# Moving half of the memory sums into the feed-forward sweep, and giving the last two batch pairs a sweep each

## The chip, the cores and the metric

One core of one Trainium2 chip runs the whole program. The metric is device time in microseconds (us) of one execution. PE is the matrix engine, DVE the vector engine, ACT the scalar engine, POOL the GpSimd engine, SP the engine that issues the transfers. Each engine works through its own instructions strictly in the order of the program; between engines there are only semaphores.

## The reference

Eight batches, eight heads, 576 tokens, 64 dimensions, 32 memory slots. An attention over memory slots, then a gated feed-forward layer (512 to 1536 to 512) on all 4608 tokens:

```python
a = exp(phi - max(phi, axis=seq)); a = a / (sum(a, axis=seq) + 1e-9)
k_m = einsum('bhsm,bhsd->bhmd', a, k)
v_m = einsum('bhsm,bhsd->bhmd', a, v)
s = q @ k_m.T / sqrt(64)
attn = softmax(s); out = attn @ v_m          # one row of 512 per token: x
xn = x / sqrt(mean(x * x) + 1e-6) * rms_g
g = xn @ w_gate; val = xn @ w_val
return (g * sigmoid(g) * val) @ w_out
```

The three weights arrive as 64-bit floats, everything else as 32-bit ones.

## The kernel before, in words

**Splitting.** The large products are made from values split into a high and a low part, each in a format that PE reads at full rate: high by high, high by low, low by high, three matmuls for one. A split is a cast on ACT (the high part: xh, hh, ath, wh, oh) and a subtraction on DVE or POOL (the low part: xl, hl, atl, wl, ol).

**Weights.** `convert` turns a block of 64-bit weights (128 x 512, tile raw) into 32-bit ones with integer steps on DVE: the exponent (tile ex, L345 to L358), the mantissa (tile mi, L365, L369), their product (tile w, L385); one activation on ACT and the split stand between. There are 36 blocks, named by kind and number: 0 is gate, 1 value, 2 output. Each split block is also written to DRAM, and `reload` fetches it from there when it is needed again.

**Batches in pairs.** Pair 0 holds batches 0 and 1, and so on to pair 3; pairs 2 and 3 are the late batches 4 to 7.

**Part 1** (up to line 819) makes k_m and v_m of all eight batches: the max of phi over tokens (mc, L509; transposed as mt on PE, L516; max mx; transposed back as mr, L533; subtracted, L542), the exponential into e_bd, its products with keys and values (kvp, L583) and with ones (L598), the division, and transposes (kvt). POOL adds several of the exponentials first (es), so that fewer products with ones are needed. For pairs 0 and 1 it also makes the queries' transposes (qtp), the scores (S, L718), the attention a, and the norm: `x_steps` transposes a (tp, L184), multiplies by a Gram matrix of v_m (xp, L235), sums on DVE (L248), takes the inverse root in 25 small DVE steps (`fin`, L259 to L276), and spreads the result over the transposed attention (rp on PE, L204, and L212 on DVE). The late batches' v_m and Gram matrices go to DRAM.

**Part 2** has 48 iterations, one for each block of 128 hidden columns and each pair. An iteration multiplies v_m with the gate and value block (vp, L852, 12 matmuls; evacuated as xh on ACT and xl on DVE), multiplies the attention with the result (pg and pv, L888, 48 matmuls; silu sg on ACT, product hf on DVE, hh on ACT, hl on POOL), and after every second iteration adds the output block for nine token tiles (po, L930, 54 matmuls; sum acc on DVE, first by a copy, L935, then by an addition, L937). Sweep 1, the first 24 iterations, takes pairs 0 and 1 in turn; sweep 2 takes pairs 2 and 3 in turn, with the weights read back once. Inside sweep 1 lie most of the weight conversions, the eight attention steps (`attend_steps`) of pairs 2 and 3, and the norms of both.

**Order.** Every step has a number, its place in iterations, from a table (`PRM`): `ev` collects pairs of place and function, sorts them and calls them. From that trace a scheduler sets each engine's order, which is then fixed. PSUM, eight banks, is given out by pools; part 2's tiles take the banks that part 1 gives back.

## Time and profile before

| | |
|---|---|
| runs, median (lowest to highest) | 919.43 us (917.98 to 920.09) |
| profiled execution, its span | 921.27 us, 919.5 us |
| PE busy | 843.9 us, 92% |
| DVE busy | 633.7 us, 69% |
| ACT busy | 382.2 us, 42% |
| POOL busy | 287.7 us, 31% |
| moved by DMA | 106.41 MB, mean 116 GB/s |

PE reads as busy while one of its matmuls is in flight, also where the next has to wait a little; so the share of 92% does not mean that only 8% could be saved. A row of the timeline gives start, duration, engine, line, operation and tiles, and in brackets the idle time ahead of it with what ended it. A row of a group gives the count, the total, the mean of one in ns, and the idle time ahead.

### The profile page before, as it was taken

How to read it: one execution, taken by the hardware profiler on the slowest of the kernel's cores; microseconds unless marked ns; L12 is line 12 of the kernel's file. 1: busy time of each engine (PE TensorE's matmuls, PEld its weight loads, DVE VectorE, ACT ScalarE, POOL GpSimd, SP SyncE). 2: the span in 40 equal slices, each digit the busy share in tenths (PEclk: the TensorE clock that was granted, in tenths of full speed). 3: DMA queues.
4: the chain of work that ended last, by engine and by line, in shares of the span. 5: the costliest groups of instructions: out<-in, count | busy, mean ns of one | idle time of the engine just before them, and what ended most of it. 6: DMA issues, size and time to landing. Idle time of an engine off the chain costs nothing.

```text
span 919.5 us, 15815 instructions
## 1 busy us (share of the span) xinstructions
PE 843.9 (92%) x6207; PEld 750.0 (82%) x6207; DVE 633.7 (69%) x1094; ACT 382.2 (42%) x647; POOL 287.7 (31%) x242
## 2 busy tenths in 40 slices
PE   4899675799989999999999999999999999999997
PEld 3778664788878798888887897799989999999996
DVE  5587969998998978978964664655455454554543
ACT  2566333645545445555542352333324233242330
POOL 3465735331432332333332151222111121121120
PEclk9799876999999999999999999999999999999999
DMA  8997644443353423433323135221203012040046
GB/s 281 268 292 244 224 138 130 135 160 82 126 165 104 158 88 120 133 109 126 116 76 115 35 92 150 69 81 47 93 1 118 20 47 92 1 138 1 1 112 141
DMA packets 85666, 106.41 MB, mean 116 GB/s; under 512 B 38996, under 2 KB 56920, under 8 KB 85592
## 3 DMA queue, kind: packets, MB, share of 16 engines
q1 hardware_dynamic: 85592, 105.41, 37.8%
q8 instruction: 49, 0.80, 0.4%
q14 instruction: 25, 0.20, 0.1%
HBM read 73.93 MB, written 31.46 MB: 115 GB/s over the span
## 4 chain that ended last, share of the span: by engine, by line
PE 59%; DVE 14%; issue 5%; ACT 3%; POOL 1%; DVEq 0%; ACTq 0%; POOLq 0%
PE po L930 26%; PE pv L888 13%; PE pg L888 13%; PE vp L852 5%; DVE xl L866 2%; DVE mi L369 1%; DVE hf L897 1%; DVE w L385 1%; DVE acc L937 1%; DVE ex L352 1%; DVE ex L345 1%; DVE mi L365 1%; DVE ex L358 1%; DVE ex L357 1%; DVE acc L935 1%
## 5 line engine op out<-in xcount | busy, mean ns | idle before, releaser
L911 POOL TENSOR_TENSOR hl<-hf,hh 128x512 fp32r<-128x512 f32 (+1 forms) x96 | 139.9, 1457 | 441.8 <-ACT hh L910 439.5
L937 DVE TENSOR_TENSOR acc<-po,acc 128x512 f32<-128x512 f32 x180 | 123.1, 687 | 117.2 <-PE po L930 116.3
L930 PE MATMUL po<-oh,hh 128*128 128x512 f32 x432 | 173.4, 402 | 4.8 <-DVE ex L1005 1.9
L930 PE MATMUL po<-oh,hl 128*128 128x512 f32 x432 | 171.3, 397 | 0.0
L930 PE MATMUL po<-ol,hh 128*128 128x512 f32 x432 | 171.1, 396 | 0.0
L896 ACT ACTIVATE sg<-pg 128x256 f32<-128x256 f32 x192 | 77.4, 409 | 170.4 <-PE pg L888 146.4
L866 DVE TENSOR_TENSOR xl<-vp,xh 64x1024 fp32r<-64x1024 f32 x96 | 117.0, 1219 | 39.0 <-ACT xh L865 37.6
L865 ACT CAST xh<-vp 64x1024 fp32r<-64x1024 f32 x96 | 96.7, 1007 | 68.3 <-PE vp L852 31.3
L897 DVE TENSOR_TENSOR hf<-pv,sg 128x256 f32<-128x256 f32 x192 | 84.4, 452 | 51.3 <-PE pv L888 39.6
L910 ACT CAST hh<-hf 128x512 fp32r<-128x512 f32 (+1 forms) x96 | 64.7, 673 | 105.2 <-DVE hf L897 63.7
L888 PE MATMUL pg<-ath,xh 128*128 128x320 f32 (+1 forms) x384 | 86.3, 300 | 13.0 <-ACT xh L865 8.0
L930 PEld LDWEIGHTS po<-oh,hl 128*128 128x128 f32 x432 | 81.6, 189 | 19.5
L930 PEld LDWEIGHTS po<-oh,hh 128*128 128x128 f32 x432 | 82.0, 190 | 18.7 <-DVE acc L937 3.0
L930 PEld LDWEIGHTS po<-ol,hh 128*128 128x128 f32 x432 | 82.0, 190 | 11.3
L852 PE MATMUL vp<-wh,vm 128*128 128x256 f32 x384 | 86.3, 290 | 2.6 <-DVE xl L866 1.6
L888 PE MATMUL pv<-ath,xh 128*128 128x320 f32 (+1 forms) x384 | 85.1, 302 | 2.7 <-DVE hf L897 2.6
L888 PE MATMUL pg<-ath,xl 128*128 128x320 f32 (+1 forms) x384 | 85.0, 296 | 0.0
L888 PE MATMUL pg<-atl,xh 128*128 128x320 f32 (+1 forms) x384 | 84.6, 296 | 0.0
L888 PE MATMUL pv<-atl,xh 128*128 128x320 f32 (+1 forms) x384 | 84.3, 297 | 0.0
L888 PE MATMUL pv<-ath,xl 128*128 128x320 f32 (+1 forms) x384 | 83.8, 298 | 0.0
L888 PEld LDWEIGHTS pg<-ath,xh 128*128 128x128 f32 x384 | 63.7, 190 | 18.9 <-ACT xh L865 8.3
L852 PEld LDWEIGHTS vp<-wh,vm 128*128 128x128 f32 x384 | 66.9, 195 | 5.7 <-DVE xl L866 2.0
(131 smaller groups left out, 1393.8 us busy)
## 6 DMA issues: line engine op xcount, KB each, us to landing
kv<-in_k_dram SPq DMA_DIRECT2D x32, 288.0 KB, 6.3
kv<-in_v_dram SPq DMA_DIRECT2D x32, 288.0 KB, 6.5
out_dram<-acc SPq DMA_DIRECT2D x72, 128.0 KB, 2.4
raw<-in_moe_w_gate_dram SPq DMA_DIRECT2D x12, 512.0 KB, 3.8
raw<-in_moe_w_val_dram SPq DMA_DIRECT2D x12, 512.0 KB, 3.7
wd<-wh SPq DMA_DIRECT2D x12, 512.0 KB, 3.3
wd<-wl SPq DMA_DIRECT2D x12, 512.0 KB, 3.5
raw<-in_moe_w_out_dram SPq DMA_DIRECT2D x12, 512.0 KB, 3.6
```

The lines of the kernel that those rows point to most:

```text
L345: V.tensor_scalar(out=ex, in0=hw, scalar1=0x7FF00000, scalar2=None, op0=ALU.bitwise_and)
L352: V.tensor_scalar(out=ex, in0=ex, scalar1=float(-896 << 20), scalar2=0.0, op0=ALU.add, op1=ALU.max)
L852: nc.tensor.matmul(vp[:, cc, e, :], lhs(l), r[:, 2 * cc + e, :], start=(n == 0), stop=(n == 2),)
L865: nc.scalar.copy(xh[rows], src)
L866: nc.vector.tensor_tensor(out=xl[rows], in0=src, in1=xh[rows].bitcast(F32), op=ALU.subtract)
L888: nc.tensor.matmul(pt[:, :N], l[:, cc, b, half * P:half * P + P], r[:, b, cc, t0:t0 + n, :].rearrange("p t x -> p (t x)"), start=(m == 0), ...
L896: nc.scalar.activation(sg[:, :N], pg[:, :N], AF.Silu)
L897: nc.vector.tensor_tensor(out=hf[:, :, b, :], in0=pv[:, :N].rearrange("p (t x) -> p t x", x=64), in1=sg[:, :N].rearrange("p (t x) -> p t x ...
L910: nc.scalar.copy(hh, hv)
L911: nc.gpsimd.tensor_tensor(out=hl, in0=hv, in1=hh.bitcast(F32), op=ALU.subtract)
L930: nc.tensor.matmul(po, l[:, tt, :], r, start=(m == 0), stop=(m == 5))
L937: nc.vector.tensor_tensor(out=accs[key], in0=po, in1=accs[key], op=ALU.add)
```

## The change

Part 1 now handles pairs 0 and 1 only. The late batches' key and value sums are a new function, `late_kv`, of 19 steps, placed at iterations 1.5, 3.8, 13.5 and 15.5 of sweep 1. It works in two PSUM buffers (tag o) that the attention steps use as well, and in SBUF tiles of those steps.

The iterations are dealt anew: pairs 0 and 1 share the first 24, then pair 2 has twelve, then pair 3. The weights are read back twice. The attention steps of pair 3 and its norm move into pair 2's sweep.

Two pieces of work go to ACT: one step of each conversion's exponent (`CB`), and the copy that starts each sum (`accs`). POOL's es sums are gone from part 1 (`ESN`), all sums over tokens are made by products with ones there. The loads of part 1 stand in a fixed list. The first PSUM tiles of part 2 are asked for in the order o, v, vw. From the end of pair 0's norm on, later DVE steps are held behind it (`issue_after`). The tile w2 of the conversions has two buffers in place of three.

```diff
-WB = 3
+WB = 2
-    K_AT=[12.08, 15.05, 41.68, 67.52, 100.72, 122.69, 147.6, 167.28],
+    K_AT=[12.0, 21.0, 50.0, 60.0],
-    ESN=[3, 3, 2, 3, 3, 3, 2, 3],
+    ESN=0,
-    SU=[1.874, 3.014, 5.716, 6.6, 9.746, 12.208, 13.357, 15.533],
+    WR=2.85,
+    OR=0.4,
+    KV=[1.5, 3.8, 13.5, 15.5],
+    SU=[6.0, 7.6, 9.2, 10.8, 24.2, 25.7, 27.2, 28.7],
-    XB=[17.199, 22.916],
+    XB=[18.0, 30.2],
-    CB=0,
+    CB=1,
...
-        for b in range(B):
+        for b in range(2 * G):
             steps, post = kv_steps(b)
...
             ev += [(PRM["X_AT"][pr] + PRM["XP"] * p, f) for p, f in x_steps(
-                    pr, lambda t, pr=pr: a_tiles[pr][:, t], tile_of("tr"), tile_of("kx"))]
+                pr, lambda t, pr=pr: a_tiles[pr][:, t], tile_of("tr"), tile_of("tr" if pr else "kx"))]
         for _, f in sorted(ev, key=lambda e: e[0]):
-            f()
+            with tc.issue_after(roots[0]) if 0 in roots else nullcontext():
+                f()
+    ps.tile([P, 512], F32, tag="o", name="o_first")
+    ps.tile([P, 512], F32, tag="v", name="v_first")
+    ps.tile([P, 2, 2, 256], F32, tag="vw", name="vw_first", bufs=1)
+    UNITS = [(p, u) for u in range(NU) for p in range(G)] + [(p, u) for p in range(G, NP) for u in range(NU)]
     def where(i):
-        ps_, r = divmod(i, NU * G * 2)
-        u, r = divmod(r, G * 2)
-        pi, f = divmod(r, 2)
-        return ps_, u, ps_ * G + pi, 2 * u + f
+        pr, u = UNITS[i // 2]
+        j = 2 * u + i % 2
+        return u, pr, j, j if pr < G else NJ * (pr - G + 1) + j
...
                 if u == 0:
-                    nc.vector.tensor_copy(accs[key], po)
+                    nc.scalar.copy(accs[key], po)
...
+    def late_kv(b):
...
+        def top():
+            d["mc"] = mc = sb.tile([P, HP, M], F32, tag="la", name=f"mc{b}")
+            nc.vector.tensor_reduce(
+                out=mc, in_=d["phi"].rearrange("p hp c m -> p hp m c"), axis=AX.X, op=ALU.max
+            )
+        def turn_mc():
+            d["t"] = tp = o_tile(f"mt{b}")
+            nc.tensor.transpose(out=tp[:, :P], in_=d["mc"].rearrange("p hp m -> p (hp m)"), identity=ident)
...
+        def exp():
+            for h in range(2):
+                rows = slice(64 * h, 64 * h + 64)
+                nc.scalar.activation(late[pr][rows, :, :, 32 * h:32 * h + 32], d["phi"][rows], AF.Exp)
...
+        def mm(cc):
+            def f():
+                d["kvp"] = kvp = o_tile(f"kvp{b}_{cc}")
...
+        return [
+            lambda: (fetch_phi(), fetch_kv(0)()), top, turn_mc, top2, turn_mb, less, exp, some,
+            mm(0), sums(0), norm(0), fetch_kv(1), mm(1), sums(1), norm(1), turn, post, self_products, post2,
+        ]
...
+        if n >= NJ:
+            ev.append((i - PRM["WR"], lambda n=n: reload(0, n)))
+            ev.append((i - i % 2 - PRM["OR"] + 0.01 * (i % 2), lambda n=n: reload(2, n)))
+    for a, p in enumerate(PRM["KV"]):
+        ev += place(p, PRM["KO"], late_kv(2 * G + a))
```

Three places show what this does to the engines' order. A row is line, operation, tiles and shape; the first digit in a tile's name is the pair, the batch or the iteration, in ex, mi and w it is the kind and the next one the block. The first place is DVE at the end of part 1, in pair 1's inverse root (rinv1, u1). Before:

```order
L274 TENSOR_TENSOR u1_1666<-rinv1_71 128x9
L275 TENSOR_TENSOR u1_1666<-u1_1666,m1_1660 128x9
L276 SCALAR_TENSOR_TENSOR rinv1_71<-u1_1666,rinv1_71 128x9
...
L212 TENSOR_TENSOR at1_1503<-at1_1503,rp1_0_1760 128x1024
L212 TENSOR_TENSOR at1_1503<-at1_1503,rp1_4_1770 128x1024
L385 TENSOR_TENSOR w1_1_1735<-mi1_1_1731,ex1_1_1726 128x512
L212 TENSOR_TENSOR at1_1503<-at1_1503,rp1_8_1776 128x256
L345 TENSOR_SCALAR ex2_0_1828<-raw_20_1724 128x512
...
L385 TENSOR_TENSOR w2_0_1839<-mi2_0_1833,ex2_0_1828 128x512
L866 TENSOR_TENSOR xl0_1823<-vp0_1809,xh0_1822 64x1024
```

and with the change:

```order
L358 SCALAR_TENSOR_TENSOR ex2_1_1614<-raw_21_1285,ex2_1_1614 128x512
L986 TENSOR_REDUCE mc4_1695<-phi4_1656 128x128
L276 TENSOR_TENSOR u1_1401<-u1_1401,m1_1395 128x9
L385 TENSOR_TENSOR w2_1_1631<-mi2_1_1625,ex2_1_1614 128x512
L277 SCALAR_TENSOR_TENSOR rinv1_75<-u1_1401,rinv1_75 128x9
L345 TENSOR_SCALAR ex0_2_1714<-raw_02_1481 128x512
L365 TENSOR_SCALAR mi0_2_1719<-raw_02_1481 128x512
L275 TENSOR_TENSOR u1_1401<-rinv1_75 128x9
L347 TENSOR_SCALAR ex0_2_1714<-ex0_2_1714 128x512
L369 SCALAR_TENSOR_TENSOR mi0_2_1719<-raw_02_1481,mi0_2_1719 128x512
```

The root's steps, which stood together, now have conversions and a late batch's max between them; the conversion that stood behind the root is gone from there.

The second place is PE, from the end of pair 1's norm to the first gate matmul. Before:

```order
L204 MATMUL rp1_8_1776<-ident_58,rinv1_71 128x128
L652 MATMUL kvt7_1755<-vt7_1766 64x64 x4
L852 MATMUL vp0_1809<-wh0_1363,vm0_456 128x256
L852 MATMUL vp0_1809<-wl0_1364,vm0_456 128x256
...
L888 MATMUL pg0_00_1849<-ath0_1393,xh0_1822 128x256 x2
```

and with the change:

```order
L205 MATMUL rp1_8_1425<-ident_58,rinv1_75 128x128
L850 MATMUL vp0_1454<-wh0_554,vm0_388 128x256
L850 MATMUL vp0_1454<-wl0_555,vm0_388 128x256
L850 MATMUL vp0_1454<-wh0_554,vm0_388 128x256 x2
...
L850 MATMUL vp0_1454<-wh0_554,vm0_388 128x256
L992 MATMUL mt4_1747<-ident_58,mc4_1695 128x128
L886 MATMUL pg0_00_1494<-ath0_883,xh0_1467 128x256 x2
```

The first v_m product stands directly behind the spreading of the norm in both; batch 7's transposes have left, and batch 4's first one has come in ahead of the gate matmul.

The third place is DVE in sweep 1, at iterations 7 and 8. Before:

```order
L897 TENSOR_TENSOR hf6_1_3012<-pv6_10_3014,sg6_10_3027 128x5x64
L897 TENSOR_TENSOR hf6_1_3012<-pv6_11_3062,sg6_11_3075 128x5x64
L866 TENSOR_TENSOR xl8_3143<-vp8_3045,xh8_3142 64x1024
L385 TENSOR_TENSOR w2_5_3476<-mi2_5_3470,ex2_5_3459 128x512
L897 TENSOR_TENSOR hf7_0_3123<-pv7_00_3125,sg7_00_3138 128x4x64
L345 TENSOR_SCALAR ex0_6_3571<-raw_06_3225 128x512
L365 TENSOR_SCALAR mi0_6_3587<-raw_06_3225 128x512
L897 TENSOR_TENSOR hf7_0_3123<-pv7_01_3177,sg7_01_3190 128x4x64
L352 TENSOR_SCALAR ex0_6_3571<-ex0_6_3571 128x512
L369 SCALAR_TENSOR_TENSOR mi0_6_3587<-raw_06_3225,mi0_6_3587 128x512
L866 TENSOR_TENSOR xl8_3143<-vp8_3045,xh8_3142 64x1024
L937 TENSOR_TENSOR acc0_0_2109<-po5_0_2874,acc0_0_2109 128x512
```

and with the change:

```order
L358 SCALAR_TENSOR_TENSOR ex0_5_2735<-raw_05_2592,ex0_5_2735 128x512
L385 TENSOR_TENSOR w0_5_2762<-mi0_5_2741,ex0_5_2735 128x512
L345 TENSOR_SCALAR ex1_5_2798<-raw_15_2676 128x512
L365 TENSOR_SCALAR mi1_5_2811<-raw_15_2676 128x512
L347 TENSOR_SCALAR ex1_5_2798<-ex1_5_2798 128x512
L864 TENSOR_TENSOR xl8_2890<-vp8_2802,xh8_2889 64x1024
L369 SCALAR_TENSOR_TENSOR mi1_5_2811<-raw_15_2676,mi1_5_2811 128x512
L935 TENSOR_TENSOR acc0_0_1760<-po5_0_2625,acc0_0_1760 128x512
L358 SCALAR_TENSOR_TENSOR ex1_5_2798<-raw_15_2676,ex1_5_2798 128x512
L864 TENSOR_TENSOR xl8_2890<-vp8_2802,xh8_2889 64x1024
L385 TENSOR_TENSOR w1_5_2817<-mi1_5_2811,ex1_5_2798 128x512
L345 TENSOR_SCALAR ex2_4_2929<-raw_24_2744 128x512
```

Both have conversions there. Before, one step or two of a conversion stand between the sweep's own rows; now parts of three conversions follow one another, with the two halves of xl8 among the steps of one.

262 lines of the change are left out of this document (179 added, 83 removed).

## The prediction

> **What bounds the kernel now.** I read the windows view first, with the span cut where the matmuls change their rate: up to the first gate matmul, the first sweep in three pieces, its tail, the second sweep, the end.
>
> ```profile
> core 0: us, PE busy (x) PEld busy (x) DVE busy (x) ACT busy (x) POOL busy (x), PEclk, DMA share, GB/s
> 0.00:158.10 158.10, 114.78 (x1485) 97.77 (x1485) 115.86 (x240) 71.04 (x128) 80.26 (x87) 0.85 0.74 222
> 158.10:292.10 134.00, 119.60 (x832) 109.07 (x833) 125.81 (x202) 71.28 (x118) 43.18 (x31) 0.97 0.43 132
> 292.10:319.40 27.30, 23.17 (x147) 19.26 (x146) 26.88 (x44) 12.58 (x19) 10.86 (x8) 0.94 0.53 170
> 319.40:539.80 220.40, 214.88 (x1470) 190.45 (x1469) 171.43 (x305) 106.76 (x181) 73.51 (x58) 1.00 0.32 101
> 539.80:603.20 63.40, 60.28 (x395) 52.00 (x394) 35.02 (x75) 19.25 (x34) 18.12 (x17) 0.97 0.43 111
> 603.20:900.00 296.80, 296.80 (x1825) 270.13 (x1824) 151.19 (x222) 100.53 (x167) 60.20 (x42) 1.00 0.18 56
> 900.00:919.50 19.50, 14.41 (x63) 11.33 (x61) 7.52 (x12) 0.79 (x2) 1.57 (x1) 0.97 0.66 153
> ```
>
> From 603.2 to 900 us PE never idles, so there a matmul's price is the distance from its start to the next one's. The timeline of that stretch has it:
>
> ```profile
> 700.07 0.39 PE L930 MATMUL po<-oh,hh 128*128 128x512 f32 x1
> 700.30 0.39 PE L930 MATMUL po<-ol,hh 128*128 128x512 f32 x1
> 703.56 0.28 PE L852 MATMUL vp<-wh,vm 128*128 128x256 f32 x1
> 703.68 0.29 PE L852 MATMUL vp<-wl,vm 128*128 128x256 f32 x1
> ```
>
> po 0.2325, vp 0.119 and, from the same view, gate and value 0.131 us on average: the 588 po (three groups like the first below), 1009 gate and value and 228 vp in that window make 296, its length. The groups of that window (first row), and of the first sweep's:
>
> ```profile
> L930 PE MATMUL po<-oh,hl 128*128 128x512 f32 x196 | 77.4, 395 | 0.0
> ...
> L930 PE MATMUL po<-oh,hh 128*128 128x512 f32 x182 | 73.7, 405 | 4.7 <-DVE ex L1005 1.9 <-DVE acc L937 1.9 <-ACT qT L982 0.9
> L888 PE MATMUL pg<-ath,xh 128*128 128x256 f32 (+1 forms) x192 | 44.4, 305 | 13.0 <-ACT xh L865 8.0 <-ACT sg L896 5.0
> L852 PE MATMUL vp<-wh,vm 128*128 128x256 f32 x192 | 42.0, 292 | 1.6 <-DVE xl L866 1.6
> ```
>
> In the first sweep 546 po (three such groups) cost 127, 1152 gate and value (six) 151, 288 vp (192 and 96) 34, and 23 for the late batches' scores and norm sums: 335. The sweep takes 381.7, so 46 us are lost, though PE reads as busy for 357.7. By piece the loss is 24 of the first 134.0 us (PE work 110), 7 of the next 27.3 (20) and 15 of the last 220.4 (206). DVE is busy 94%, 98% and 78% of these pieces: where it is full PE waits, and where its work is 171.4/206 = 0.83 of PE's, 7% of PE's time is still lost. After the sweep 8, 1 and 5.4 us are lost.
>
> So the span is 158 to the first gate matmul, 701 of PE work, and 46 + 8 + 1 + 5.4 of loss: 919.5. The profiled run took 921.3, the median of the runs is 919.4; I put the sum for the span down as the time of a run.
>
> Before 158.1 us PE does 84 us of work by such prices. What sets its end, in the timelines:
>
> ```profile
> 97.28 0.22 PE L718 MATMUL S<-km,qT 128*64 128x64 f32 x1
> 120.68 1.97 PE L184 MATMUL tp<-ident,a 128*128 128x128 f32 x8
> 138.41 0.17 DVE L259 TENSOR_SCALAR m<-ssq 128x9 f32<-128x9 f32 x1
> 142.56 0.17 DVE L276 SCALAR_TENSOR_TENSOR rinv<-u,rinv 128x9 f32<-128x9 f32 x1
> 147.23 0.58 PE L852 MATMUL vp<-wh,vm 128*128 128x256 f32 x1 [0.87 <-DVE at L212]
> 149.61 1.49 DVE L352 TENSOR_SCALAR ex<-ex 128x512 int32<-128x512 int32 x1
> 155.82 1.21 DVE L866 TENSOR_TENSOR xl<-vp,xh 64x1024 fp32r<-64x1024 f32 x1
> 158.12 0.80 PE L888 MATMUL pg<-ath,xh 128*128 128x256 f32 x2 [7.96 <-ACT xh L865]
> 158.43 0.41 DVE L352 TENSOR_SCALAR ex<-ex 128x512 int32<-128x512 int32 x1
> ```
>
> A chain: pair 1's last score, 23 us to its attention a, 18 us of transposes and norm sums, 4.2 us of inverse root, then 15.5 us to the gate matmul. In the last stretch one weight conversion stands ahead of xl on DVE, with steps of 1.49 us that take 0.41 at 158.43.
>
> **The change part by part.** *Late batches leave part 1.* One batch costs PE 72 kvp at 0.060, four transposes, self products, two max transposes and sums: 4.3 + 0.8 + 0.45 + 0.6 + 0.3 = 6.4 us (rows of the kind below; 2.94/49 = 0.060). Four batches, 25.6 us, go from a stage where PE is half idle into one where it is the floor: PE work after the first gate matmul becomes 701 + 26 = 727.
>
> ```profile
> 93.41 2.94 PE L583 MATMUL kvp<-kv,e_bd 128*64 128x128 f32 x49
> L509 DVE TENSOR_REDUCE mc<-phi 128x128 f32<-128x1152 f32 (+1 forms) x9 | 17.3, 1936 | 7.8 <-DMA phi<-in_phi_dram 7.8
> L542 DVE TENSOR_TENSOR phi<-phi,mr 128x1152 f32<-128x1152 f32 (+1 forms) x9 | 11.0, 1218 | 11.2 <-PE mr L533 11.2
> 146.26 5.96 POOL L224 TENSOR_TENSOR atl<-at,ath 128x512 fp32r<-128x512 f32 x4
> ```
>
> The change pays, then, only as far as the first gate matmul comes earlier than 158.1 and the losses behind it shrink: 26 us have to be won.
>
> *The first gate matmul.* Loads bound it from below: 16 of 32 key and 16 of 32 value loads of 288 KB and four phi go, about 12 MB of 35 in this stretch, and the rest, 23 MB at 222 to 264 GB/s, needs some 90 to 105 us. Pair 1's last scores follow its last query and the late key blocks, which stand behind pair 0's norm sums in PE's order; I put them at 99, about where they are now. From there to a took 23 us while DVE was busy 20 of 21 us and POOL ran sums for late batches; without those, 12 to 23, taken 14: 113. Transposes and norm sums took 18 with late batches' matmuls between them; alone, with two PSUM buffers instead of four, 14: 127. Then the inverse root: its 25 small steps took 4.2 in a row, but DVE's new order (the first of the three places shown above) holds between them the rest of the first output block, three whole conversions and the max of batch 4. A conversion's six steps cost 3 x 0.42 + 3 x 0.68 = 3.3 where nothing disturbs DVE (row at 158.43 for the short kind), so 0.7 + 3 x 3.3 + 2.2 + 4.2 = 17: 144. Nothing may start without it, since the rows behind it on PE are rp1 and vp0. Against that the conversion no longer stands ahead of xl0: rp, vp0, two halves of xh and one of xl, 1.3 + 2.5 + 2.0 + 1.2 with waits, is 9 where it was 15.5. **First gate matmul at 153**, bounds 140 (a at 105, three conversions waiting for their loads elsewhere) and 162 (23 us to a, phi of batch 4 late, which DVE meets in the middle of the root).
>
> *DVE in the first sweep.* It now does 324 us there (125.8 + 26.9 + 171.4):
>
> ```profile
> L937 DVE TENSOR_TENSOR acc<-po,acc 128x512 f32<-128x512 f32 x73 | 49.9, 684 | 30.1 <-PE po L930 29.8
> L385 DVE TENSOR_TENSOR w<-mi,ex 128x512 f32<-128x512 f32 x31 | 27.7, 894 | 2.2 <-POOL wl L403 0.7 <-POOL ol L403 0.7
> L369 DVE SCALAR_TENSOR_TENSOR mi<-raw,mi 128x512 f32<-128x512 uint32 x31 | 26.6, 858 | 0.0
> L357 DVE TENSOR_SCALAR ex<-ex 128x512 int32<-128x512 int32 x31 | 18.6, 601 | 0.0
> L352 DVE TENSOR_SCALAR ex<-ex 128x512 int32<-128x512 int32 x31 | 18.3, 591 | 0.0
> L935 DVE COPY acc<-po 128x512 f32<-128x512 f32 x18 | 12.2, 677 | 0.1
> L1017 DVE TENSOR_REDUCE sm<-ex 128x18 f32<-128x576 f32 x8 | 6.0, 749 | 2.2 <-ACT ex L1012 2.1
> ```
>
> A conversion of seven steps is 153/31 = 4.9 us. One step of 0.6 goes to ACT in each, and about four conversions now come before the sweep: 27 x 4.35 = 117, 36 less. The 18 first copies, 12.2, go to ACT. Four of eight attends leave, 13 (each 4 steps of 0.45 and 0.75 + 0.54 + 0.26). Each late batch brings a max 2.2, a subtraction 1.35 and some 3 of small steps: four make 25, after the part of batch 4 that lies earlier. 324 - 36 - 12 - 13 + 25 = 288. PE work in the sweep becomes 335 - 8 (four attends) + 26 = 353. DVE stands at 288/353 = 0.82 of PE's work, as in the last piece now, which lost 7%: **25 us**. On top: the conversions no longer lie evenly. One w2 buffer fewer and the new events leave iterations 4 to 7 without one and put six between hf7 and hf8 (the third place shown begins there). Four such clumps follow, 26 to 34 us of DVE against 15 to 18 of PE; the one piece of that kind now, 292.1 to 319.4, lost 7. Half of that pattern is in the 7% already; I add 6: **31**. From below 20 (only the clumps cost, at half of 7 each, and 6), from above 42, where each clump costs DVE's excess less about 5 us for which PE has other rows.
>
> ACT takes 27 activations of 0.63 and 18 copies of about 0.7, 30 us, and stands at 191 of 382 now: I cost that at nothing, hidden by ACT's own idle half, though hh is queued behind them, and po waits for hh.
>
> *Sweeps of pairs 2 and 3.* Weights are read back twice instead of once; one iteration moves 1.5 MB in 14 us, 107 GB/s, where 222 was reached: hidden. Four attends and pair 3's norm now lie in pair 2's sweep, which has DVE half free; the 9 us lost after 539.8, mostly for pair 3's norm, become 6 (bounds 3 and 12). The tail stays at 5.4.
>
> **Sum:** 153 + 727 + 31 + 6 + 5.4 = 922, against 919.4: the gain in part 1 and on DVE, 23 us, is eaten by the 26 us that move under PE's floor.
>
> **The rivals.** *Faster, 904.* The clumps run undisturbed. The mechanism is POOL against DVE: while POOL splits at in one row of 5.96 us from 146.26, a DVE step takes 1.49, otherwise 0.41. If POOL is quiet in the clumps, six steps cost 3.3 instead of 4.35, 27 conversions 28 us less, and DVE at 260/353 loses about 18 instead of 31; with part 1's chain undisturbed as well, the gate matmul comes at 148. 148 + 727 + 18 + 6 + 5.4 = 904. For it: the low row; against: POOL splits each conversion's result and two hl per iteration in the same clumps, and the mean of such a step over the sweep is 0.6, not 0.4. It decides from 20 us of loss down. The Trainium skill (SBUF — State Buffer, Who interferes with whom) says that DVE steps with two SBUF inputs, or in a two-port mode, contend with GpSimd for a shared port pair, one blocking the other; the rows of 1.49 beside 0.41 agree.
>
> *Clearly slower, 938.* Late batches as they behaved in part 1: each is a chain mc, mt, mx, mb, mr, exp, kvp, kvt in PE's in-order queue, and whatever stands behind waits too.
>
> ```profile
> PE mt L516 <- DVE mc L509: 10.0, 3, 5.0
> PE mr L533 <- DVE mb L528: 6.4, 4, 3.8
> L1012 ACT ACT_TABLE_LOAD x8 | 10.3, 1283 | 0.8 <-issue 0.4 <-DVE ex L1005 0.2
> ```
>
> 3.3 for a mt and 1.6 for a mr is 5 for each batch, 16 to 20 in all: 922 + 16 = 938. For it: mt4 stands directly ahead of the first gate matmul. Against: iterations lie between a step and its matmul, as far as the order shows. It decides if PE's waits name mt, mr, kvp or kvt with more than 2 us per batch. Each late batch also costs ACT two table loads around its exp, 1.28 each. The Trainium skill (ScalarE: Activation LUTs, What ACT_TABLE_LOAD costs) gives 1.28 us and a drain of 1.38 more for a switch; the row has the first part, and no row here shows the second. By it eight switches would take ACT 21 us instead of 10.
>
> *The dealt banks do nothing.* vp waited 0.87 us for DVE at L212. That is all the order of the PSUM pools can win at the start, and it is inside the 9 us above.
>
> **How the numbers follow.** 45% for the forecast, which spreads from 912 to 932 with the start of the sweep; 30% for the faster rival and what lies below; 25% for the slower. A change of 0.2%, 1.8 us, can be told from none. Of the forecast's band a little over a quarter lies below 917.6 and as much within 1.8 us of 919.4: faster 0.30 + 0.12, same 0.12, slower 0.25 + 0.21. Range: earliest gate matmul with the small loss, 140 + 727 + 20 + 6 + 5.4 = 898, and the latest with the large, 162 + 727 + 42 + 6 + 5.4 = 942; both ends at once are unlikely, and the low one more so than the slower rival: 901 to 942.
>
> **What would show it.** The first pg at 150 to 156, with the inverse root's first and last rows 15 us apart on DVE. The first sweep's 24 iterations 375 to 395 long, DVE busy under 80% of it, long iterations at 8 to 9 and 12 to 13. No wait over 5 us from a late batch's tile. From iteration 24 on 14 us each. I am wrong if the gate matmul comes before 145, if the sweep loses under 20, or if pair 2's sweep waits for reloaded weights.

## The result, and the profile after: 979 us, ratio 1.064

The changed kernel took 979.17 us (median, 975.72 to 980.36) beside 919.76 for the kernel before on the same chip: ratio 1.0637, 95% interval 1.0613 to 1.0662. Slower was forecast as about as likely as faster, but by 2 us and at most 22, not by 59. Times here are of fast executions alone; one slow execution of experiment 9's first kernel, of 2102 us, is not counted. The profiled execution has a span of 978.6 us; its windows, cut at the first gate matmul, at iteration 24 (end of sweep 1) and at the ends of the other two sweeps:

```profile
core 0: us, PE busy (x) PEld busy (x) DVE busy (x) ACT busy (x) POOL busy (x), PEclk, DMA share, GB/s
0.00:168.40 168.40, 104.51 (x1206) 89.34 (x1206) 98.67 (x229) 66.00 (x120) 46.49 (x61) 0.71 0.53 163
168.40:587.90 419.50, 384.48 (x2714) 340.77 (x2715) 302.86 (x500) 216.62 (x359) 142.36 (x107) 0.96 0.38 123
587.90:785.20 197.30, 192.63 (x1333) 171.27 (x1332) 104.70 (x187) 86.91 (x142) 48.14 (x37) 0.99 0.46 136
785.20:960.90 175.70, 175.70 (x1063) 159.40 (x1063) 82.76 (x123) 63.32 (x106) 37.87 (x29) 1.00 0.31 98
960.90:978.60 17.70, 12.92 (x57) 10.13 (x55) 7.05 (x11) 0.73 (x1) 1.57 (x1) 0.94 0.60 134
```

With the prediction's prices for a matmul the PE work in the last four windows is 353, 185, 175 and 13. What is left of each is loss:

| | before | forecast | after | after less forecast |
|---|---|---|---|---|
| first gate matmul | 158.1 | 153 | 168.4 | +15.4 |
| PE work from there on | 701 | 727 | 726 | -1 |
| loss in sweep 1 | 46 | 31 | 66.5 | +35.5 |
| loss behind it | 14.4 | 11.4 | 17.7 | +6.3 |
| span | 919.5 | 922 | 978.6 | +56 |

So the PE work was sized rightly. The miss is the loss in sweep 1, and the gate matmul, which came later than before instead of earlier. Its chain in the timeline (PE and DVE rows):

```profile
115.30 1.27 PE L712 MATMUL S<-km,qT 128*64 128x64 f32 x36 [0.30 <-ACT qT L699]
126.07 1.12 PE L185 MATMUL tp<-ident,a 128*128 128x128 f32 x4 [9.51 <-POOL a L752]
143.80 0.17 DVE L260 TENSOR_SCALAR m<-ssq 128x9 f32<-128x9 f32 x1
148.36 2.08 DVE L986 TENSOR_REDUCE mc<-phi 128x128 f32<-128x1152 f32 x1
158.32 0.16 DVE L277 SCALAR_TENSOR_TENSOR rinv<-u,rinv 128x9 f32<-128x9 f32 x1
158.63 1.94 PE L205 MATMUL rp<-ident,rinv 128*128 128x128 f32 x8 [15.40 <-DVE rinv L277]
161.21 0.47 PE L205 MATMUL rp<-ident,rinv 128*128 128x128 f32 x1 [0.64 <-DVE at L213]
161.34 0.56 PE L850 MATMUL vp<-wh,vm 128*128 128x256 f32 x1
168.45 0.79 PE L886 MATMUL pg<-ath,xh 128*128 128x256 f32 x2 [4.09 <-ACT xh L863]
```

From pair 1's last score (the last start in the first row's group, 116.3) to the gate matmul it is 52.1 us; the prediction had 54 (14 + 14 + 17 + 9; measured 9.8, 17.7, 14.5 and 10.1). All of the error lies ahead of these rows: the last score came at 116.3, not at 99. The longest wait of the queue that issues the loads (total, count, longest), and then rows of that queue and of DVE:

```profile
SPq L299 <- PE kvp L583: 38.5, 3, 33.4
```
```profile
75.44 0.33 SPq L299 DMA_DIRECT2D kv<-in_k_dram  x1
78.30 14.44 SPq L299 DMA_DIRECT2D q<-in_q_dram  x8
92.79 0.59 SPq L299 DMA_DIRECT2D raw<-in_moe_w_gate_dram  x1
98.58 0.43 DVE L345 TENSOR_SCALAR ex<-raw 128x512 int32<-128x512 int32 x1 [11.61 <-DMA raw<-in_moe_w_gate_dram]
105.43 0.42 DVE L615 TENSOR_TENSOR kb<-kvp,im 128x256 f32<-128x256 f32 x1
```

The queue stands for 33.4 us, from 42.0 to 75.4: batch 3's keys wait for a buffer that batch 2's kvp frees, and that kvp stands behind pair 0's norm sums on PE. So pair 1's queries go out from 78 on and the weight block at 92.8. DVE waits for that block with batch 3's division behind it, and makes one conversion and half of the next before it divides (kb, at 105.43); batch 3's transposes and pair 1's scores follow. Batch 3's own products end on PE only at 99.2, since its keys were late, so of this delay some 6 us are DVE's.

In sweep 1 PE's waits are spread, and none is large:

```profile
PE pv L886 <- DVE hf L895: 11.2, 5, 3.6
PE pg L886 <- ACT xh L863: 4.7, 3, 4.1
...
PE kvp L1030 <- ACT e_late L1015: 2.1, 2, 1.3
```

Listing for each matmul how much later the next one starts than its price allows, 40 of the 66 us are steps over 0.4 us (before: 28 of 46), and 26 are many small ones (18). How a stall makes some of the second kind is seen where pv waited longest, in the timeline of POOL, DVE and PE:

```profile
273.95 2.03 POOL L909 TENSOR_TENSOR hl<-hf,hh 128x640 fp32r<-128x640 f32 x1
275.92 2.02 POOL L966 MEMSET e_late<- 128x2304 f32 x1
274.59 3.64 DVE L345 TENSOR_SCALAR ex<-raw 128x512 int32<-128x512 int32 x1
278.15 1.48 DVE L365 TENSOR_SCALAR mi<-raw 128x512 int32<-128x512 int32 x1
280.62 0.40 DVE L895 TENSOR_TENSOR hf<-pv,sg 128x256 f32<-128x256 f32 x1
276.12 0.46 PE L886 MATMUL pg<-ath,xl 128*128 128x320 f32 x2
281.07 0.90 PE L886 MATMUL pv<-ath,xh 128*128 128x320 f32 x2 [3.62 <-DVE hf L895]
281.77 0.73 PE L886 MATMUL pv<-atl,xh 128*128 128x320 f32 x2
```

This is the clump between iterations 7 and 8, just ahead of the third place of the order shown above, whose first row stands at 286.04. One conversion step takes 3.64 us in place of 0.41, for as long as POOL runs a split and then clears e_late, a tile that the change added; hf stands behind it on DVE and PE behind hf. Seven of the profiled kernels have this order, and the step takes 3.63 to 3.64 us in each. After 3.6 us of idleness PE's next matmuls take 0.73 a pair where the same shape took 0.46. The slow stretch is longer than the stall: a vp at 286.57 still takes 0.41, one at 287.12 takes 0.29. The granted clock from the stall on is 0.66:

```profile
177.00:277.50 100.50, 94.73 (x727) 86.00 (x725) 60.63 (x86) 60.22 (x99) 39.62 (x28) 0.98 0.30 99
277.50:285.90 8.40, 4.83 (x19) 4.79 (x20) 8.40 (x19) 3.40 (x7) 3.31 (x3) 0.66 0.52 158
```

Two pages of the Trainium skill bear on these rows. The Trainium skill (SBUF — State Buffer, Who interferes with whom) says that a DVE step in a two-port mode and a GpSimd instruction exclude each other, whichever starts first, for the whole instruction; the step of 3.64 us ends 0.3 us after POOL's second instruction (275.92 + 2.02), which agrees. The Trainium skill (TensorE: Matmul & The Clock Gate, Part 1) says that the array's clock falls to half after an idle window of about 3.4 us and comes back after a busy one as long. These rows agree with the fall, with 3.6 us of idleness ahead of the slow pairs; the way back took longer here, since the vp at 286.57 is slow 5.5 us after PE's restart at 281.07.

### The profile page after: what moved, and what is told of

It reads as the page before. It is cut to its first block, busy times and chain, and to the rows that moved or that the text cites. A ratio compares the mean times of both kernels' runs of the same rounds, so it can differ in the third digit from the quotient of the medians.

```text
span 978.6 us, 16269 instructions
## 1 busy us (share of the span) xinstructions
PE 870.2 (89%) x6367; PEld 770.9 (79%) x6367; DVE 596.0 (61%) x1048; ACT 433.6 (44%) x725; POOL 276.4 (28%) x232
## 4 chain that ended last, share of the span: by engine, by line
PE 64%; DVE 19%; ACT 6%; DMA 4%; issue 4%; POOL 1%; SPq 1%; DVEq 0%; ACTq 0%; POOLq 0%
PE po L928 26%; PE pv L886 12%; PE pg L886 12%; PE vp L850 5%; DVE xl L864 3%; PE xp L236 2%; DVE ex L345 2%; DVE acc L935 2%; DVE w L385 2%; DVE mi L365 2%; DVE ex L358 1%; DVE ex L347 1%; DVE mi L369 1%; PE tp L185 1%; ACT xh L863 1%
## 5 line engine op out<-in xcount | busy, mean ns | idle before, releaser
L894 ACT ACTIVATE sg<-pg 128x256 f32<-128x256 f32 x192 | 78.3, 411 | 162.4 <-PE pg L886 132.5
L928 PE MATMUL po<-oh,hh 128*128 128x512 f32 x324 | 132.1, 408 | 7.7 <-DVE ex L1155 3.1
L928 PE MATMUL po<-ol,hh 128*128 128x512 f32 x324 | 129.7, 400 | 0.0
L928 PE MATMUL po<-oh,hl 128*128 128x512 f32 x324 | 129.0, 399 | 0.0
L886 PE MATMUL pv<-ath,xh 128*128 128x320 f32 (+1 forms) x384 | 86.4, 306 | 11.2 <-DVE hf L895 11.2
L850 PE MATMUL vp<-wh,vm 128*128 128x256 f32 x384 | 83.8, 291 | 3.1 <-DVE xl L864 1.6
L886 PE MATMUL pg<-atl,xh 128*128 128x320 f32 (+1 forms) x384 | 86.3, 300 | 0.0
L928 PEld LDWEIGHTS po<-oh,hh 128*128 128x128 f32 x324 | 61.9, 191 | 21.0 <-DVE acc L935 4.7
L886 PEld LDWEIGHTS pv<-ath,xh 128*128 128x128 f32 x384 | 64.9, 194 | 16.4 <-DVE hf L895 11.4
L928 PEld LDWEIGHTS po<-oh,hl 128*128 128x128 f32 x324 | 61.8, 191 | 14.5
```

The source lines that it names most:

```text
L850: nc.tensor.matmul(vp[:, cc, e, :], lhs(l), r[:, 2 * cc + e, :], start=(m == 0), stop=(m == 2),)
L886: nc.tensor.matmul(pt[:, :N], l[:, cc, b, half * P:half * P + P], r[:, b, cc, t0:t0 + n, :].rearrange("p t x -> p (t x)"), start=(m == 0), ...
L894: nc.scalar.activation(sg[:, :N], pg[:, :N], AF.Silu)
L928: nc.tensor.matmul(po, l[:, tt, :], r, start=(m == 0), stop=(m == 5))
```

## The experiments

Four theories were in play: the late batches cost more in the sweep than their matmuls (theirs), the conversions come in clumps because w2 has two buffers (clumps), the two moves to ACT cost more than ACT's idle half (ACT), and part 1 is held up by its new order, in the loads or on DVE (order). All medians stand beside about 920 for the kernel before and 979 for the change. Experiments 1 to 3 have two executions each, the others four to ten. A time within a profile is of one execution: over five kernels whose part 1 is nearly that of the kernel before (its own, three of experiment 6 and that of experiment 5), the first gate matmul lies between 155.4 and 159.9, so differences of 4 us there are not clear of chance.

**1. The change without the late sums.** They are left out (zeros stand for them), everything else stays.

```diff
+        return [filled]
...
-        ev += place(p, PRM["KO"], late_kv(2 * G + a))
+        ev += place(p, PRM["KO"][:1], late_kv(2 * G + a))
```

`filled`, the only step left, writes the zeros.

> The changed kernel without the late batches' sums: their k_m, v_m and Gram matrices are set to zero, so the sums, their loads, exponentials and transposes are left out. PE work falls by 25.6 us, DVE's by 25, ACT's by about 20. Theory C (clumps): the sweep is 419.5 - 26 = 394 with a loss of 60 or more. Rival K (late batches): the loss goes back to 45 or less, the sweep takes 372 to 380, the run 930 to 940.

936.47 us, ratio 1.0175 (1.0142 to 1.0207). The sweep falls from 419.5 to 377.0:

```profile
169.90:546.90 377.00, 353.05 (x2277) 315.55 (x2278) 282.90 (x447) 193.77 (x332) 119.66 (x91) 0.97 0.32 106
```

The late sums cost 42.5 us there, where their PE work is 25.6. And without them the rest of the change still loses 49.5 of the sweep (377.0 less 327.5 of work), with DVE at 282.90, below the forecast's 288: DVE's lighter load did not bring the loss down. The result lies between the two expectations: sweep and run fall into rival K's ranges, the loss of 49.5 is over its 45 and under theory C's 60.

**2. Their matmuls alone.** The late batches' matmuls stay, on constant operands and into the same PSUM buffers; loads, max, exponential, divisions and copies are left out.

```diff
...
+            filled, n0, pe_mt("mt", 0), n0, pe_mt("mr", 0), n0, n0, n0,
+            pe_mm(0), pe_sums(0), n0, n0, pe_mm(1), pe_sums(1), n0, pe_turn, n0, pe_self, n0,
```

> The changed kernel with the late batches' matmuls and transposes kept in sweep 1 at their places and in their PSUM tiles, but on constant operands: their loads, max, exponential, division and copies are left out, and k_m, v_m and Gram matrices are zero. Without any of it the sweep took 377.0, with all 419.5, and the PE work between them is 25.6. Theory W (waits of the chain, and DVE's and ACT's work): the sweep takes 398 to 406, that is the 25.6 and little more. Rival O (the two o banks, which po needs too, held by late tiles, and PE's order): 412 or more.

965.46 us, ratio 1.0497 (1.0476 to 1.0518); the sweep is 408.2.

```profile
166.30:574.50 408.20, 379.55 (x2715) 338.16 (x2716) 283.19 (x447) 194.99 (x331) 118.55 (x89) 0.98 0.30 98
```

Of the 42.5 us, 31.2 come with the matmuls: 25.6 of work and 5.6 more, which standing in order and holding the banks would explain, but the run does not tell the two apart. 11.3 come with the chain of the other engines. The sweep lies between both expectations (398 to 406, and 412 or more). PE's wait for hf follows the chain: 11.2 us in the sweep of the change, 5.5 here, 3.5 in experiment 1.

**3. The chain with fewer matmuls.** 16 of each late batch's 72 kvp products, the rest of the chain whole.

```diff
-                for c in range(NT):
+                for c in (0, NT - 1):
```

> The changed kernel with only 16 of 72 key and value products of each late batch, so that their k_m and v_m are sums over two of nine token groups; loads, max, exponential, division, transposes and copies are all kept. PE work falls by 56 x 0.058 x 4 = 13 us. Theory W (the chain's waits): the sweep takes 405 to 408, 13 less than 419.5, the 17 us beyond PE's work staying. Rival M (the kvp matmuls themselves, placed between pg and po, stall on their loads): 400 or less.

970.89 us, ratio 1.0556 (1.0535 to 1.0577), sweep 407.8: 11.7 shorter for about 13 us of matmuls left out. What the chain loses stays, as theory W had it (405 to 408); this agrees with experiment 2.

**4. Three w2 buffers in the change.** The buffer's space comes from two small late tiles, which share others' space instead.

```diff
-WB = 2
+WB = 3
-            d["vt"] = vt = sb.tile([P, HP, 64], F32, tag="lc", name=f"vt{b}")
+            d["vt"] = vt = sb.tile([P, HP, 64], F32, tag="la", name=f"vt{b}")
...
```

> The changed kernel with three w2 buffers for the conversions in place of two; room is made by letting the late batches' v tiles use the tiles la and lb. On DVE six conversions between hf7 and hf8 become three or fewer at a place. Theory C (clumps): the first sweep loses 66 us because the conversions stand in clumps; spread, it loses 40 to 45, and the run takes 954 to 960. Rival K (late batches): the loss comes from the late batches' chain of small steps in PE's order; then the sweep stays within 5 us of 419.5, the run at 975 to 980.

978.67 us, ratio 1.0635 (1.0616 to 1.0655): no gain as a whole, and the theory that spread conversions would win some 20 us falls here. The sweep is 7 shorter (412.5), but the gate matmul comes at 176.7, 8 later: the last score is 3.5 later, and one more conversion stands ahead of xl0, so that the stretch from the first vp to the gate matmul takes 11.9 in place of 7.1.

**5. Two w2 buffers in the kernel before**, the same single number the other way round.

```diff
-WB = 3
+WB = 2
```

> The kernel before with two w2 buffers in place of three, nothing else. On DVE the conversions then stand in clumps as in the changed kernel: none at iterations 5 and 6, three at 9, 12, 17, four at 20, where they were one or two each. Theory C (clumps): the sweep takes 390 to 400 in place of 381.7, the run 928 to 938. Rival: a clump costs nothing beyond its work while other iterations have DVE free; the run stays at 918 to 922.

938.69 us, ratio 1.0199 (1.0174 to 1.0223). Beside the before's sweep, in one row (158.1 to 539.8, first fence), this one's:

```profile
158.10:539.80 381.70, 357.65 (x2445) 318.78 (x2446) 324.12 (x548) 190.62 (x318) 127.55 (x96) 0.98 0.37 117
```
```profile
155.40:556.60 401.20, 364.30 (x2446) 324.09 (x2447) 327.66 (x548) 191.11 (x318) 129.13 (x96) 0.96 0.36 111
```

DVE has the same 548 instructions and 3.5 us more to do, yet the sweep is 19.5 longer, at the upper end of theory C. PE's waits for DVE ahead of po (for ex and for acc) are 13.3 us there, and 3.8 before. How DVE's work lies costs more here than how much it is; the prediction had 6 for it.

**6. The two moves to ACT, alone.** In the kernel before: both, the first copy of each sum alone, the clamp step alone; and in the changed kernel both undone.

```diff
-                    nc.vector.tensor_copy(accs[key], po)
+                    nc.scalar.copy(accs[key], po)
...
-    CB=0,
+    CB=1,
```

> The kernel before with two parts of the change alone: one step of each conversion's exponent on ACT, and the copy that starts each sum on ACT. DVE in the first sweep does 324 - 18 - 12 = 294 us in place of 324. Theory: the first 134 us of the sweep, where DVE was busy 94% and 24 us were lost, lose 10 to 15 less, and the run takes 904 to 912. Rival A: ACT hands hh and silu out later, since the new steps stand ahead of them; the run takes 918 to 925.

> The kernel before with the first copy of each sum on ACT alone (18 copies in the sweep). Both ACT moves together gained 6 us. If DVE's busy time counts in proportion, the copies are 12.2 us of it in the sweep and the clamps 16: copies alone gain 2 to 3, run 916 to 918. If only the steps between po and the next bank count, the copies gain all, run 914 to 916.

> The kernel before with the clamp step of the conversions on ACT alone (27 conversions). In proportion to DVE time: gains 3 to 4, run 915 to 917. If the gain was the copies' alone: 918 to 920.

> The changed kernel with both pieces of work given back to DVE: the step of each conversion's exponent and the copy that starts each sum. DVE's work in sweep 1 rises by 16 + 12 us, ACT's falls by 17 + 10. In the kernel before, the same two moves to ACT shortened the sweep by 8 us. Theory (DVE late in clumps): the sweep takes 425 to 432, the run 985 to 990. Rival (ACT is what hands hf, xh and e_late out late now): the sweep shortens to 410 to 415, the run to 970 or less.

| | us | ratio (95%) | sweep 1 |
|---|---|---|---|
| before, both on ACT | 914.82 | 0.993 (0.9911 to 0.9949) | 373.6 |
| before, copies on ACT | 916.58 | 0.997 (0.9947 to 0.9992) | 376.0 |
| before, clamp on ACT | 916.29 | 0.9964 (0.9942 to 0.9986) | 378.5 |
| change, both back on DVE | 996.78 | 1.0838 (1.0813 to 1.0863) | 432.3 |

```profile
159.90:533.50 373.60, 355.69 (x2445) 318.08 (x2446) 297.33 (x495) 216.43 (x367) 128.33 (x96) 0.98 0.38 119
```

These two moves gain, in both kernels; the theory that they cost falls. The sizes miss the expectations: together 6 us where 8 to 16 were expected, and taking them back costs the change 17.6 where 6 to 11 were expected (12.8 in the sweep, 5.5 ahead of it). The gains add up: about 3 us each alone, as their share of DVE's time would have it, 6 together by the ratios. With 27 us less on DVE the sweep's loss fell from 46 to 38, 0.3 us for each. The kernel before with these two edits has the lowest median here, 0.7% under the kernel before.

**7. Pair 0's norm later**, so that batch 2's kvp no longer stands behind it and the loads flow on.

```diff
-    X_AT=[41.0, 84.0],
+    X_AT=[52.0, 84.0],
```

> The changed kernel with pair 0's norm sums placed 11 steps later in part 1 (52 in place of 41), so that batch 2's key products stand ahead of them on PE and free a key buffer early. Theory L (the load queue): the key loads of batch 3, and behind them pair 1's queries and the second weight blocks, stood 33.4 us behind batch 2's products; with that gone, pair 1's last scores end near 98 in place of 116.5, the first gate matmul comes at 148 to 153 in place of 168.4, and the run takes 959 to 964. Rival D (DVE): pair 1 is late because the second weight blocks' conversions stand ahead of its scores on DVE, which waited 11.6 us for their raw block; that wait ends with the load as well, but the conversions' own 9 us stay, so that the first gate matmul comes only some 8 us earlier, 160, and the run takes 970. Sweep 1 stays at 415 to 420 in both.

974.94 us, ratio 1.0589 (1.057 to 1.0607); gate matmul at 163.7. The stand did not go, it found another cause: 22.3 us, for a kvp that now waited for its exponential. The last score came only 1.5 us earlier, and the run lies above both expectations, nearer to rival D's.

**8. Batches 2 and 3 and their loads early**, pair 0's scores and norm behind them; then the same without the rule that holds later DVE steps behind pair 0's root (`issue_after`).

```diff
-    K_AT=[12.0, 21.0, 50.0, 60.0],
+    K_AT=[12.0, 21.0, 34.0, 44.0],
-    PH=[0.0, 8.0, 33.0, 43.0],
-    S_AT=[31.0, 32.5, 34.0, 35.5, 70.0, 72.0, 74.0, 76.0],
+    PH=[0.0, 8.0, 18.0, 28.0],
+    S_AT=[38.0, 39.5, 41.0, 42.5, 70.0, 72.0, 74.0, 76.0],
-    X_AT=[41.0, 84.0],
+    X_AT=[62.0, 84.0],
```

> The changed kernel with part 1 placed anew: batches 2 and 3 earlier (preparation at 18 and 28 in place of 33 and 43, products at 34 and 44 in place of 50 and 60), pair 0's scores 7 steps later and its norm at 62. On PE batch 2's products stand at row 91 in place of 188. With the norm alone placed later, SP still stood 22.6 us, since the products waited for batch 2's exponential. Theory L (the load queue): SP no longer stands more than 10 us behind batch 2's products, pair 1's last scores end at 100 or earlier, the first gate matmul comes at 145 to 152, and the run takes 955 to 962. Rival D (DVE's own list): pair 1's chain is as long as DVE's work ahead of it, 99 us busy in part 1, whatever the loads do; the first gate matmul stays at 160 or later, the run at 970 or more.

> The run part1_early with one rule of the change undone besides: DVE's steps that are called after pair 0's inverse root are no longer held behind it. In part1_early the key loads came 22 us earlier than in the changed kernel, yet pair 1's first softmax step stood at 105.9, right behind the end of pair 0's root at 105.5, while its first scores were there from 76. Theory Q (the held queue): without the rule pair 1's scores are taken in from about 80 on, its last scores end at 95 to 105, the first gate matmul comes at 150 to 160 in place of 172.4, and the run takes 965 to 972. Rival D (DVE has as much to do whatever its order): the gate matmul stays at 166 or later.

986.16 us, ratio 1.0721 (1.0704 to 1.0739), and 978.43, 1.0654 (1.0609 to 1.0699). The key loads came at 53 to 59, the queries at 59 to 78, and still the last score at 117.8: pair 0's root ended only at 105.5, and the rule kept pair 1's softmax behind it. Without the rule it came at 120.8: both theories that one queue sets it, L and Q, fall, and the results lie in rival D's ranges. The gate matmuls came at 172.4 and 168.1. This edit also moves pair 0's norm to 62, so that it lies among pair 1's scores on PE and DVE. Early keys with that norm out of the way were not run.

**9. The weights' conversions behind pair 1's softmax**, once with the change's own part 1 and once with that of experiment 8, there without the rule on pair 0's root.

```diff
-    CV2=62.0,
+    CV2=92.0,
...
+                if (pr, s) == (1, HP - 1):
+                    roots["s"] = last
...
-            with tc.issue_after(roots[0]) if 0 in roots else nullcontext():
+            with tc.issue_after(roots.get("s", roots.get(0))) if 0 in roots else nullcontext():
```

> The changed kernel with the second gate and value blocks' conversions held behind pair 1's last softmax step on DVE; their loads stay where they are. In the changed kernel they stood ahead of batch 3's division and of pair 1's softmax, and DVE waited 11.6 us for their raw block there. Theory D (DVE's order): with the wait and the 9 us of work gone from in front, pair 1's last scores end 10 to 18 us earlier than 117.5, at 100 to 107, and the first gate matmul comes at 152 to 160 in place of 168.4; the run takes 963 to 972. Theory L (the load queue): SP still stands 33 us behind batch 2's products, and pair 1's queries come at 78 to 93 as before; the last scores end at 112 or later, the gate matmul at 164 or later, the run at 974 or more.

> The run part1_early, with the second weight blocks' conversions held behind pair 1's last softmax step and the rule on pair 0's root undone, so that both the load queue and DVE's order are mended. If each of the two alone is only masked by the other, pair 1's last scores end at 90 to 100, the first gate matmul comes at 140 to 150, and the run takes 950 to 962. If something else sets part 1's end (the chain query, transpose, copy, scores, softmax, four times over), the gate matmul stays at 160 or later and the run at 970 or more.

979.25 us, ratio 1.0646 (1.0604 to 1.0688), and 980.88, 1.066 (1.0622 to 1.0698): last scores at 116.2 and 114.2, gate matmuls at 172.4 and 170.9. In the first one DVE is free ahead of batch 3's division, and waits for batch 3's products instead, whose keys are still late:

```profile
102.72 0.16 DVE L606 TENSOR_SCALAR si<-kvp 128x2 f32<-128x2 f32 x1 [11.76 <-PE kvp L598]
```

In the second one neither loads nor DVE's conversions are ahead of the scores any more, and other queues take over:

```profile
104.92 1.09 PE L205 MATMUL rp<-ident,rinv 128*128 128x128 f32 x4 [5.18 <-DVE sm L752]
113.10 1.31 PE L712 MATMUL S<-km,qT 128*64 128x64 f32 x36
127.52 1.11 PE L185 MATMUL tp<-ident,a 128*128 128x128 f32 x4 [13.12 <-POOL a L754]
```

Pair 0's spreading (rp) stands ahead of the last scores on PE, and then a waits on POOL, behind pair 0's splits and row sums. The two forms of the theory "order", loads and DVE, each fall as the only cause: with the conversions gone the late keys hold the scores, and with both gone pair 0's norm does.

**10. Pair 1's root in one piece**: part 2's steps are held behind it.

```diff
-        f()
+        with tc.issue_after(roots[1]):
+            f()
```

> The changed kernel with all DVE steps of part 2 held behind pair 1's inverse root, so that its 25 small steps stand together, as before the change. Theory (the interleaved conversions cost what they take): the root takes 4 to 5 us in place of 15.4, the first gate matmul comes 8 to 11 us earlier than 168.4, at 157 to 160; two of the conversions follow within the sweep and cost it 0 to 5 us; the run takes 970 to 974. Rival (a sum that stays): the sweep takes over in full what the root gives, and the run stays within 2 us of 979.

980.09 us, ratio 1.0648 (1.0621 to 1.0676). The root's rows stand together, 3.1 us from first to last:

```profile
148.95 0.17 DVE L260 TENSOR_SCALAR m<-ssq 128x9 f32<-128x9 f32 x1
152.03 0.17 DVE L277 SCALAR_TENSOR_TENSOR rinv<-u,rinv 128x9 f32<-128x9 f32 x1
157.12 0.56 PE L850 MATMUL vp<-wh,vm 128*128 128x256 f32 x1
170.34 0.80 PE L886 MATMUL pg<-ath,xh 128*128 128x256 f32 x2 [10.10 <-ACT xh L863]
```

The 11 us won there are gone at the last row: the conversions that left the root now stand ahead of xl0 (13.2 us from the first vp to the gate matmul, 7.1 in the change), and the norm sums ended 5 later, as the last score already had (121.5). The rival is the one that holds: the run stays within 2 us of 979.

**11. The kernel before with no late sums at all**: not loaded, not summed, zeros in their place, in part 1 or elsewhere.

```diff
-        for b in range(B):
+        for b in range(2 * G):
             steps, post = kv_steps(b)
...
```

> The kernel before, with the late batches' keys, values and phi neither loaded nor summed anywhere (zeros are written in their place), and nothing else changed: the part 1 that the change could have had at best if it had kept the old order. Theory H (the late sums were hidden in part 1, whose end is set by the chain of pair 1): first gate matmul 154 to 160 against 158.1, the sweep unchanged, run 915 to 922. Theory P (the late sums held part 1 up, as the prediction took: 9 us less from the last score to a, 4 less in the norm sums, 3 less ahead of the gate matmul): first gate matmul 138 to 148, run 900 to 910; then the later last score of the changed kernel comes from its new order of loads and steps, not from what part 1 has to do.

923.64 us, ratio 1.0037 (1.0013 to 1.0062), gate matmul at 162.3 in the profiled execution, which with 927.3 us was the slowest of ten. Some 26 of 84 us of PE's work in part 1, 12 MB of loads (94.5 MB moved in all, 106.4 before) and the chains of four batches are gone, and part 1 did not end 10 to 20 us earlier: it ended 4 us later, and 3.7 us is what this execution lies above the median. Its timeline:

```profile
76.02 0.43 DVE L345 TENSOR_SCALAR ex<-raw 128x512 int32<-128x512 int32 x1 [3.33 <-DMA raw<-in_moe_w_gate_dram]
106.75 1.66 PE L718 MATMUL S<-km,qT 128*64 128x64 f32 x36 [1.01 <-ACT qT L705]
133.00 0.17 DVE L259 TENSOR_SCALAR m<-ssq 128x9 f32<-128x9 f32 x1
133.08 0.68 DVE L385 TENSOR_TENSOR w<-mi,ex 128x512 f32<-128x512 f32 x1
147.24 0.16 DVE L276 SCALAR_TENSOR_TENSOR rinv<-u,rinv 128x9 f32<-128x9 f32 x1
162.32 0.79 PE L897 MATMUL pg<-ath,xh 128*128 128x256 f32 x2 [5.69 <-ACT xh L874]
```

Nothing of the new part 1 is in this kernel, and yet it shows two of the change's marks: the last score late (108.1, before 97.3), and the inverse root spread over 14.2 us with three conversions between its steps. The weight loads have moved up: the second gate, the second value and the first output block are loaded at 79.7, 86.3 and 92.0, where before they came at 99.0, 119.0 and 119.5. So DVE begins five conversions between 76 and 101, where before it began two by then, and pair 1's softmax stands among them; that these delay the score is read from the order, and was not tested apart. Something was won as well: from the last score to the end of the norm sums it is 24.9 us, before 41.1 (9.7 in place of 23.4 to a, 15.2 in place of 17.7 from there). The later score (11 us) and the longer root (10 us) took it back. (The longest stand of the load queue, 26.6 us, lies behind the last score, from 105.9 to 132.5, and has no part in it.) Theory P, that the gate matmul comes earlier as soon as the late sums are gone, falls; theory H comes nearest, with the gate matmul and the run 2 us over its ranges.

## Why the prediction was wrong

**"The first gate matmul at 153": failed, at the step "Pair 1's last scores ... I put them at 99, about where they are now."** They came at 116.3, and this is the whole miss of 15.4. The prediction named the late key blocks behind pair 0's norm sums, and put that wait at nothing: the load queue stood for 33.4 us there. The steps behind it held within 4 us each and within 2 as a sum: the root with its interleaved conversions 14.5 (17), the stretch to the gate matmul 10.1 (9); the norm sums, taken as 14 without the late batches' matmuls, stayed at 17.7, and a took 9.8 in place of 14. The saving that the prediction took behind the score came in good part, then, in the change and in experiment 11. What it left out is that the order ahead of the score does not stay when work leaves. Experiment 11 shows it without any of the change's new lists: as soon as the late sums leave, weight loads and conversions move up into the same in-order queues, pair 1's last score comes 11 us later, and the saving is gone. The lower bound from the loads (90 to 105) was never near to deciding. Which queue sets the last score in the new part 1 has no single answer in these runs: the five new orders of experiments 7 to 9 put it between 114.2 and 120.8. As far as their rows show, the late keys are in front in the first kernel of experiment 9, pair 0's norm in the three with early keys, and in experiment 7 late keys, pair 0's spreading and conversions together. That a better order exists is not shown, nor excluded.

**"The gain in part 1 and on DVE, 23 us": neither came.** For DVE the step that failed is the price of the loss by DVE's share ("DVE stands at 0.82 of PE's work, as in the last piece now, which lost 7%"). DVE's load fell by 21 of the 36 us forecast, from 324 to 303, from 0.97 to 0.86 of PE's work, and the loss went up from 46 to 66.5. With the late sums left out it is 283 over 327.5, also 0.86, and the loss 49.5. Where two windows of one kernel have different loss at different load, the load need not be the reason. Experiment 5 shows the order alone at work, with the load nearly unchanged.

**"The conversions no longer lie evenly ... I add 6": right mechanism, mis-sized.** Two w2 buffers alone cost the kernel before 19.5 in its sweep; taking them back in the change won 7 there and nothing in the run. Why the two differ is open. The upper bound of 42 is too low even without the late batches (49.5). The clump named between iterations 7 and 8 is the one shown above, at clock 0.66.

**The late sums in the sweep: their 25.6 us of matmuls were in the forecast, a loss of their own was not.** They cost 42.5, so 16.9 of the 35.5 us by which the sweep's loss was missed are theirs (5.6 + 11.3 by experiment 2).

**"Clearly slower, 938": the nearest rival, right in size for the late sums and wrong in its rows.** It put 16 us on the late chain's waits, named mt, mr and kvp; 16.9 were measured, but not as waits of PE for their tiles: kvp waited 2.1 and mr 1.1. As far as PE's waits show, it was work of DVE, ACT and POOL placed ahead of hf and xh, and steps in PE's order. The rival was built as 922 + 16 from a sum that already held the 23 us of gain; without that gain it would have been about 960.

**The loss in sweep 1, put together.** 46 before, less 8 for the moves to ACT is 38; the change without its late sums has 49.5; the late matmuls bring 5.6 beyond their work and the chain 11.3, which makes 66.4. The sum has to come out, since its terms are differences of the same runs. The 11.5 between 38 and 49.5 is what is left for two w2 buffers and the new order, and no run measures it by itself.

**"I cost that at nothing" for ACT: held**; the moves gained 6 us in the kernel before.

**"Faster, 904": refuted.** POOL was not quiet in the clumps; DVE's six steps of a conversion took 4.6 us on average in the sweep (980, 809, 798, 768, 705 and 573 ns by the groups of L385, L345, L369, L358, L365 and L347), where 3.3 was the rival's price and 4.35 the forecast's.

**"The dealt banks do nothing": not tested apart**; the first vp starts 0.13 us behind the last rp (rows at 161), so nothing waited there for a bank.

**"Sweeps of pairs 2 and 3"**: forecast 6 of loss before the tail, measured 13, and 4.7 in the tail. No row in PE's waits there names a reloaded weight; the largest is again the inverse root (rp for rinv, 1.9 us). What the rest of the 13 is made of was not tested.

Of its own tests, the prediction said it would be wrong if the gate matmul came before 145 or the sweep lost under 20: it was wrong on the other side of both, which it had not named. Its first mark, the root's rows 15 us apart, came true (14.5) and was no proof: they do so in experiment 11 too, and setting them together (experiment 10) won nothing.

## What to carry to other kernels

Before pricing what a stage gains when work leaves it, ask whether that work lies on the chain that sets the stage's end; leaving it out altogether is the cheapest test, and here it would have shown 26 us of moved PE work with no gain to pay for it. A stage where PE is half idle can be the cheap place for work, and one where PE reads as busy for 94% (357.7 of 381.7 us) the dear one: 25.6 us of matmuls with their chain cost 42.5 there. A stall costs more than its length where the matmuls behind it run slow, as those behind the 3.6 us shown above did. Where a scheduler or in-order queues fill gaps, count on what moves up into them, and price clumps by the stall they make on the bottleneck engine, not by an engine's mean share.

## What the runs showed of the hardware that was not expected

A single DVE step of 128 x 512 took 3.64 us while POOL ran two instructions one behind the other, where the same kind took 1.49 beside one split and 0.41 otherwise. The second of the two was a MEMSET, an instruction with no input. That a MEMSET alone holds such a step up, and does not hold up every step, is seen in experiment 4:

```profile
287.40 2.04 POOL L966 MEMSET e_late<- 128x2304 f32 x1
287.39 0.69 DVE L385 TENSOR_TENSOR w<-mi,ex 128x512 f32<-128x512 f32 x1
288.11 1.61 DVE L345 TENSOR_SCALAR ex<-raw 128x512 int32<-128x512 int32 x1
```

Beside the same MEMSET the product of two tiles takes 0.69, and the TENSOR_SCALAR takes 1.61 and ends 0.3 us after the MEMSET. In the changed kernel with both pieces of work back on DVE (experiment 6) the same kind of step takes 1.66 beside it.

PE's granted clock in part 1 went down with the work that left it: 0.85 before, 0.71 with the change, and in experiment 11:

```profile
0.00:162.30 162.30, 91.94 (x1033) 76.46 (x1033) 103.97 (x236) 62.69 (x116) 65.44 (x78) 0.72 0.57 170
```

The first transposes of pair 0's attention show it, in the kernel before and in experiment 11:

```profile
75.11 0.66 PE L184 MATMUL tp<-ident,a 128*128 128x128 f32 x4
```
```profile
83.45 1.97 PE L184 MATMUL tp<-ident,a 128*128 128x128 f32 x8 [8.98 <-POOL a L758]
```

Four in 0.66 us there, eight in 1.97 here, behind 9 us of idleness. So part of what leaves PE came back here as slower matmuls. That this set the end of part 1 is not shown.
